# Loads of broadcast decays by halves of the partitions, a reordered token load and two filler products in a fused SSD and MoE kernel

## The chip, the core and the metric

The kernel runs on one core of one Trainium2 chip. The time is device microseconds from launch to end; the span in a profile is from the program's first to its last instruction and is some 1.8 us shorter. Names of engines: PE is TensorE, PEld its weight loads, DVE is VectorE, ACT is ScalarE, POOL is GpSimd, SP the engine that issues most transfers; "SPq" and the like are an engine's sequencer, which issues transfers.

## The reference

A chunked state-space block (Mamba2 SSD) is followed by a mixture of four small two-layer networks:

```python
# attention: x (4, 8, 768, 32), a (4, 8, 768), B and C (4, 8, 768, 16), float32
log_a = np.log(np.clip(a, 1e-06, 1.0))
for c in range(nc):                                   # chunks of 32 tokens
    cum = np.cumsum(la, axis=-1)
    L = np.exp(cum[:, :, :, None] - cum[:, :, None, :]) * causal
    M = np.einsum('bhin,bhjn->bhij', Cc, Bc) * L
    y[:, :, sl] = einsum(M, xc) + einsum(Cc, state) * decay_to_i
    state = decay_full * state + sum over tokens of B x decay_from_j
# mixture: N = 3072 tokens, D = 256, 4 experts, F = 1024
for e in range(E):
    out += p[:, e:e + 1] * (np.maximum(x @ w1[e], 0.0) @ w2[e])
```

The kernel uses chunks of its own, 128 tokens each: 24 of them (chunk 0 to 23), in six blocks (k) of four. The mixture's first products need only chunks 0 and 1; chunks 2 and 3 are computed between them, and the others beside the rest of the mixture. The mixture runs through slices of weights (n = 0, 1, 2, ..., 48 in all); the first two by plain products (lines L618 and L635 of the kernel), the others by a Strassen-like scheme (L569 and L654), which needs sums of weights made by POOL.

## The kernel before

The parts that the change and the argument touch. The decays of a chunk are stored once to DRAM in a cut form `acut_d` [2, 24, 4, 192] and read back with every row repeated over 64 partitions, so that one scan on DVE can make the matrix L (called LT):

```python
    def load_rows(c):                                   # B and C of a chunk, turned
        xb = load.tile([P, OCT + P], FP32, tag="xb", name="xb", bufs=4)
        ...
    def load_x(c, queue=None):                          # its tokens: two transfers of 64 rows
        ...
    def load_decays(c):
        ab = load.tile([P, NQ, TRI], FP32, tag="ab", name="ab")
        nc.sync.dma_start(
            out=ab.rearrange("p q s -> p (q s)"),
            in_=acut_d[:, real(c)].rearrange("t q s -> t (q s)").unsqueeze(1).to_broadcast(
                [NT, HALF, NQ * TRI]))                  # NT = 2, HALF = 64, NQ * TRI = 768
    ...
    def decay_part(c, part):                            # L395
        ...
            nc.vector.tensor_tensor_scan(out=LT[...], data0=s["a"][i], data1=own_i..., ...)
        if part == 1 and c < NCH - CPB:
            nc.gpsimd.tensor_mul(s["MT"][...], halves(c)[...], s["LT"][...])       # L400
    ...
    def turn(n, w=4):                                   # products of ones that only keep PE busy
        for _ in range(n):
            t = ps_att.tile([P, w, P], FP32, tag="att", name="t")
            nc.tensor.matmul(out=t, lhsT=ones, rhs=ones.unsqueeze(1).to_broadcast([P, w, P]), ...)
```

The opening, in the order in which the instructions are written (each engine keeps that order):

```python
    turn(1); turn(1, 2)
    spread(0, banks); turn(1, 3); masks(0)
    scores([0], homes); decays(0); aside(0, 3); store_decays(0)
    masks(1); spread(1, banks); masked([0], (2, 0, 1)); clip_first(nc.gpsimd, 2)
    load_rows(2); load_w1(1); store_decays(1); turn_gates(ps_att, "att")
    load_decays(3)
    outputs([0], ATT); scores([1], ...); decays(1); aside(1, 3)
    load_x(2); load_rows(3); load_w2(0); load_x(3)
    ...                                                 # chunks 2 and 3, first plain products
    load_chunk(4)                                       # rows, tokens, decays, heads
```

## Time and profile before

| | before |
|---|---|
| time, median of 3 runs | 669.06 us (667.31 to 671.33) |
| span of the profiled run | 663.2 us (its time: 664.98 us) |
| PE busy | 641.2 us, 97% of the span |
| PE idle | 22.0 us |
| decays `ab` | 21 loads of 384 KB |

From the page of the kernel before: the span, PE's busy time, then rows of 40 slices of 16.6 us each, where a digit is tenths (PE busy, the clock granted to PE, the busy share of the 16 transfer engines), and the chain of work that ended last:

```profile
span 663.2 us, 10731 instructions
...
PE   8696999999999999999999999999999999999997
...
PEclk8798999999999999999999999999999999999999
DMA  6767754878546486854477855568754687248101
...
PE 77%; DMA 17%; SPq 3%; DVE 2%; issue 1%; POOL 0%; ACT 0%; POOLq 0%; DVEq 0%
```

Apart from the last slice, everything that is not 9 in the rows of PE and its clock lies in the first four slices, 66 us. After them, PE is full in this row. The chain has 17% of its length in transfers. A chain share is not a gain: a link of the chain can be long while PE works beside it.

### The profile page before, as it was taken

Reading aid. Unit: us, or ns where it says so; the run is one execution under the profiler, and the core shown is the slowest. Engines: PE = TensorE matmul, PEld = TensorE weight load, DVE = VectorE, ACT = ScalarE, POOL = GpSimd, SP = SyncE. Lnnn points to the kernel's source line nnn. Section 1 sums busy time; section 2 is a strip of 40 time slices with the busy share of each in tenths; the row PEclk is TensorE's granted clock in tenths of the full one; section 3 lists DMA queues with packets and bytes.
Section 4 is the critical chain, followed back from the end, with each engine's and each line's share of the span. In section 5 each row is a group of like instructions: output and inputs, shape, how many; then the busy total and the mean of one; then the engine's idle time right before and its main releaser. Section 6 shows DMA issues by size and latency. Waiting matters only on the chain.

```text
span 663.2 us, 10731 instructions
## 1 busy us (share of the span) xinstructions
PE 641.2 (97%) x4085; PEld 549.3 (83%) x4085; DVE 470.5 (71%) x814; ACT 124.1 (19%) x314; POOL 106.3 (16%) x169
## 2 busy tenths in 40 slices
PE   8696999999999999999999999999999999999997
PEld 5575888788888888888888888887888888888886
DVE  6353698878868777876687876777767675765665
ACT  4001122121212122122122112212121212111111
POOL 6464455512000001000000100000100000100001
PEclk8798999999999999999999999999999999999999
DMA  6767754878546486854477855568754687248101
GB/s 180 201 211 240 228 181 151 254 284 252 158 139 189 148 267 204 240 141 147 142 205 198 259 164 157 156 178 267 243 173 144 231 270 252 100 129 222 31 1 32
DMA packets 103504, 122.14 MB, mean 184 GB/s; under 512 B 29810, under 2 KB 88478, under 8 KB 103454
## 3 DMA queue, kind: packets, MB, share of 16 engines
q1 hardware_dynamic: 100402, 111.60, 56.8%
q0 software_dynamic: 2432, 9.50, 3.7%
q8 instruction: 32, 0.52, 0.3%
q10 hardware_dynamic: 620, 0.37, 0.2%
q14 instruction: 18, 0.15, 0.1%
HBM read 108.56 MB, written 12.88 MB: 183 GB/s over the span
## 4 chain that ended last, share of the span: by engine, by line
PE 77%; DMA 17%; SPq 3%; DVE 2%; issue 1%; POOL 0%; ACT 0%; POOLq 0%; DVEq 0%
PE acc L654 36%; PE X L569 21%; PE Y L569 16%; DMA ab<-acut_d 6%; DMA wt<-in_w_dram 5%; DMA wt<-w_d 3%; DMA xb<-in_xbc_dram 2%; PE g L429 1%; PE y L488 1%; PE y L466 1%; SPq L136 1%; DMA acut_d<-a_cut 1%; PE acc L635 1%; DVE z L581 0%; DVE hT L598 0%
## 5 line engine op out<-in xcount | busy, mean ns | idle before, releaser
L581 DVE TENSOR_TENSOR z<-Y,snap 128x512 f32<-128x512 f32 x138 | 94.9, 688 | 140.6 <-PE Y L569 75.3
L654 PE MATMUL acc<-hT,wt 128*128 128x256 f32 x736 | 181.0, 379 | 0.0
L576 ACT COPY snap<-X 128x512 f32<-128x512 f32 x138 | 80.8, 586 | 438.8 <-PE X L569 438.8
L654 PEld LDWEIGHTS acc<-hT,wt 128*128 128x128 f32 x736 | 139.8, 190 | 19.0
L654 PE MATMUL acc<-h,wt 128*128 128x256 f32 x552 | 143.6, 383 | 0.0
L569 PE MATMUL X<-yS,wt 128*128 128x256 f32 x552 | 142.6, 381 | 0.0
L569 PEld LDWEIGHTS X<-yS,wt 128*128 128x128 f32 x552 | 105.4, 191 | 14.7 <-issue 0.3
L654 PEld LDWEIGHTS acc<-h,wt 128*128 128x128 f32 x552 | 103.1, 190 | 15.0
L569 PE MATMUL Y<-yT,wt 128*128 128x256 f32 x368 | 95.7, 383 | 6.0 <-DVE z L581 6.0
L591 DVE SCALAR_TENSOR_TENSOR h<-z,gate 128x512 f32<-128x512 f32 x138 | 99.0, 717 | 3.2
L569 PEld LDWEIGHTS Y<-yT,wt 128*128 128x128 f32 x368 | 69.1, 191 | 17.5 <-DVE z L581 7.0
L598 DVE TENSOR_TENSOR hT<-h,hT 128x512 f32<-128x512 f32 x92 | 67.0, 728 | 1.8
L598 DVE TENSOR_TENSOR hT<-h,h 128x512 f32<-128x512 f32 x92 | 61.9, 714 | 1.1
L569 PE MATMUL X<-yT,wt 128*128 128x256 f32 x184 | 47.4, 380 | 3.2 <-issue 1.7
L395 DVE TENSOR_TENSOR_SCAN LT<-ab,own_i 128x384 f32<-128x384 f32 x42 | 39.3, 948 | 13.4 <-DMA ab<-acut_d 13.4
L569 PE MATMUL Y<-yS,wt 128*128 128x256 f32 x184 | 47.2, 379 | 0.0
L591 DVE SCALAR_TENSOR_TENSOR h<-X,gate 128x512 f32<-128x512 f32 x50 | 34.5, 689 | 14.7 <-PE X L618 9.0
L569 PEld LDWEIGHTS X<-yT,wt 128*128 128x128 f32 x184 | 34.7, 190 | 8.9 <-issue 4.3
L400 POOL TENSOR_TENSOR MT<-xb,LT 128x128 f32<-128x128 f32 x20 | 9.9, 495 | 195.9 <-PE Y L569 96.3
L569 PEld LDWEIGHTS Y<-yS,wt 128*128 128x128 f32 x184 | 35.0, 190 | 4.8
L381 POOL TENSOR_TENSOR cts<-xb,dec 128x128 f32<-128x128 f32 x20 | 9.4, 490 | 156.6 <-DVE dec L378 77.2
L441 DVE TENSOR_TENSOR MT<-g,LT 128x192 f32<-128x192 f32 x94 | 26.0, 347 | 3.9 <-PE g L429 3.8
(103 smaller groups left out, 349.9 us busy)
## 6 DMA issues: line engine op xcount, KB each, us to landing
wt<-in_w_dram SPq DMA_DIRECT2D x112, 256.0 KB
wt<-w_d SPq DMA_DIRECT2D x40, 640.0 KB
wt<-w_d SPq DMA_DIRECT2D x40, 512.0 KB
ab<-acut_d SPq DMA_DIRECT2D x21, 384.0 KB
gate<-p_d SPq DMA_DIRECT2D x23, 256.0 KB
w_d<-wt POOLq DMA_DIRECT2D x8, 640.0 KB, 6.8
wt<-in_w_dram SPq DMA_DIRECT2D x40, 128.0 KB
xb<-in_xbc_dram SPq DMA_DIRECT2D x38, 128.0 KB
```

What stands on the lines that cost most here:

```text
L136: queue_.dma_start(out=halves(c)[HALF * t:HALF * t + HALF, :, OX[t]:WX - N * t], in_=src[:, :, t * DM // 2:WX])
L381: nc.gpsimd.tensor_mul(cts, s["xb"][:, OCT:], dec)
L395: nc.vector.tensor_tensor_scan(out=LT[:, i * w:i * w + w], data0=s["a"][i], data1=own_i.rearrange("p q h i -> p (q h i)")[:, :w], initial=0.0,
L400: nc.gpsimd.tensor_mul(s["MT"][:, :, 0:2, HALF:], halves(c)[:, :, OB:].rearrange("p h (q t n) -> p q h t n", q=NQ, t=NT)[:, :, :, 0], s["L ...
L429: nc.tensor.matmul(out=g[:, P * h:P + HALF * h], lhsT=s["btm"][k, h].rearrange("p t j -> p (t j)"), rhs=s["xb"][k, OCT + HALF * h:OCT + P] ...
L441: nc.vector.tensor_mul(s["MT"][:, q, :, :HALF], s["g"][q], s["LT"][:, q])
L569: nc.tensor.matmul(out=f[bank][:, j], lhsT=wt1[n][:, w, j * P:j * P + P], rhs=rhs, start=(i in (1, 2, 5) and j == 0), stop=(j == JJ - 1), ...
L576: nc.scalar.copy(out=s, in_=first[n]["X"])
L581: nc.vector.tensor_add(z, first[n]["Y"], first[n][i])
L591: nc.vector.scalar_tensor_tensor(out=h, in0=first[n][src], scalar=0.0, in1=g.unsqueeze(1).to_broadcast([P, JJ, HB]), op0=ALU.max, op1=ALU. ...
L598: nc.vector.tensor_sub(h[o], h[x], h[y])
L654: nc.tensor.matmul(out=acc[k, u][:, half], lhsT=w2_op(n, w)[:, j], rhs=rhs[:, j], start=(begins and j == 0), stop=(n % SPB == SPB - 1 and ...
```

## The change

Its intent: the decays come by one transfer for each of the two groups of heads (64 partitions each) instead of one for both; the tokens of chunk 2 and the rows of chunk 3 go in front of the decays of chunk 3; and two more products of ones fill places of the opening where PE had nothing to do, to keep its clock up.

```diff
     def load_decays(c):
         ab = load.tile([P, NQ, TRI], FP32, tag="ab", name="ab")
-        nc.sync.dma_start(
-            out=ab.rearrange("p q s -> p (q s)"),
-            in_=acut_d[:, real(c)].rearrange("t q s -> t (q s)").unsqueeze(1).to_broadcast(
-                [NT, HALF, NQ * TRI]))
+        for t in range(NT):
+            nc.sync.dma_start(
+                out=ab[HALF * t:HALF * t + HALF].rearrange("p q s -> p (q s)"),
+                in_=acut_d[t, real(c)].rearrange("q s -> (q s)").partition_broadcast(HALF))
...
     scores([0], homes)
+    turn(1, 2)
     decays(0)
...
     turn_gates(ps_att, "att")
-    load_decays(3)
+    turn(1, 2)
     outputs([0], ATT)
...
     load_x(2)
     load_rows(3)
+    load_decays(3)
     load_w2(0)
```

## The prediction

> **What bounds the kernel now.** I read the page first: the span is 663.2 us and TensorE (PE) is busy 641.2 us of it, so from far away the kernel is bound by matmuls, and all that a change of loads can give back is PE's idle time (663.2 - 641.2 = 22 us) and what PE loses at a low clock. The row PEclk has low digits only in the first slices, and the chain that ended last is 77% PE and 17% DMA. So I went to the opening, the first 70 us, with the timeline of PE and of VectorE (DVE), the waits, and a table of windows. Lines of three engines' timelines (DVE, then PE, then GpSimd, which the trace calls POOL), all those of PE with over 1 us of idle time before them after the start, and one plain line:
>
> ```profile
> 20.80 0.69 DVE L591 SCALAR_TENSOR_TENSOR h<-Y,gate 128x512 f32<-128x512 f32 x1 [0.70 <-PE Y L618]
> 24.51 1.81 DVE L395 TENSOR_TENSOR_SCAN LT<-ab,own_i 128x384 f32<-128x384 f32 x2 [3.02 <-DMA ab<-acut_d]
> ...
> 62.92 0.96 DVE L395 TENSOR_TENSOR_SCAN LT<-ab,own_i 128x384 f32<-128x384 f32 x1 [8.23 <-DMA ab<-acut_d]
> ...
> 26.58 1.09 PE L488 MATMUL y<-MT,xb 64*32 64x144 f32 x32 [5.81 <-POOL MT L400]
> 29.22 3.78 PE L618 MATMUL X<-yT,wt 128*128 128x256 f32 x8
> ...
> 46.00 1.99 PE L618 MATMUL Y<-yT,wt 128*128 128x256 f32 x8 [1.03 <-DVE h L591]
> 64.52 2.08 PE L569 MATMUL Y<-yT,wt 128*128 128x256 f32 x4 [5.16 <-DVE z L581]
> ...
> 25.42 1.11 POOL L400 TENSOR_TENSOR MT<-xb,LT 128x128 f32<-128x128 f32 x1 [10.84 <-DMA xb<-in_xbc_dram]
> ```
>
> The columns are start, length, engine, line, operation, tiles, form, count, and in brackets the idle time before and who ended it. The reader sees three stalls of PE: 5.81, 1.03 and 5.16 us, 12.0 us together. The first goes back to GpSimd (POOL), which waited for the tokens of the third chunk (chunk 2) until 25.4; the other two go back to DVE, which stood in a scan of LT waiting for the decays `ab` of chunks 4 and 5 until 44.3 and 62.9, with the next h and z of PE queued behind it. The waits say the same in total, on the engines and on the issuing queue (columns: us, times, longest):
>
> ```profile
> DVE LT L395 <- DMA ab<-acut_d: 13.4, 3, 8.2
> POOL MT L400 <- DMA xb<-in_xbc_dram: 10.8, 1, 10.8
> ...
> SPq L136 <- DMA ab<-acut_d: 23.2, 5, 5.8
> SPq L175 <- DMA ab<-acut_d: 20.4, 8, 3.2
> ```
>
> The stalls also cost clock. Columns: window, length, busy time and count of each engine, granted clock, DMA share, GB/s:
>
> ```profile
> 20.00:25.00 5.00, 0.77 (x4) 0.34 (x2) 1.28 (x3) 0.00 (x0) 0.00 (x0) 0.94 0.35 101
> 25.00:30.00 5.00, 3.42 (x50) 2.92 (x51) 2.29 (x6) 1.28 (x6) 4.35 (x7) 0.50 0.80 251
> 30.00:35.00 5.00, 5.00 (x15) 3.96 (x14) 0.87 (x2) 0.00 (x0) 4.69 (x7) 0.54 0.89 234
> 35.00:40.00 5.00, 5.00 (x53) 4.11 (x52) 3.89 (x5) 1.10 (x6) 4.43 (x7) 1.00 0.50 160
> ```
>
> The trace's clock records are half speed from 10.73 to 17.55, from 24.38 to 34.62 and from 61.93 to 68.75 us, and full otherwise until the end. And 20 to 25 us has PE idle with DMA only 0.35 busy: nothing computes, and most transfer engines do nothing either, while the loads that everybody waits for are in flight. That is a transfer spread over too few engines. The packets of 3072 bytes are `ab`'s alone (128 a load, one a partition): those of the first load start at 13.44 and end at 23.94 us, with a median of 121 ns each. 128 x 0.121 = 15.5 us of packet time within 10.5 us of clock is fewer than two engines at a time. All 21 loads take 8.5 to 12.6 us so.
>
> **What the Trainium skill says.** The page "DMA: Bandwidth & Descriptors", section "Why a DMA increments its semaphore by 16 and not by 1", says that a transfer uses the largest number of engines up to 16 that divides the slowest dimension of both sides. The source of `ab` is 2 x 64 (a repeat) x 768, so two engines; the trace agrees, as just computed. Its section "Queues, rings and completion order" says that each engine works through its ring of a queue in order. The trace agrees: transfers issued right behind the first `ab` (token loads, w2) landed 11 to 12 us after their issue, at 24.4 to 28 us, where those just before it took 3.5 to 4.7 us; a transfer over 16 engines is complete only when its parts on the two loaded ones are. The same page, "Rules for kernel authors", advises not to split a transfer into disjoint halves of the partitions, as both halves use the same engines. That is no objection here: each half has 64 rows outermost on both sides, so it goes from 2 engines to 16. "TensorE: Matmul & The Clock Gate", Part 1, tells of an idle window that halves the clock and a busy one that restores it; the records above agree (half speed after the idle stretches of 5.81 and 5.16 us, for 10.2 and 6.8 us).
>
> **The change part by part.** (a) Decays by two transfers of 64 x 768. Each of 16 engines gets 8 packets instead of two getting 64: 8 x 0.121 = about 1 us in place of 10.5. No byte is saved; 384 KB a chunk as before, and 21 more issues of some 0.55 us on a queue engine that computes nothing. What is behind in the rings no longer waits. The queue keeps eight transfers in flight (each waits for the eighth before it), so the halves also use up slots, but each lands quickly.
>
> (b) The load of chunk 3's decays goes behind the tokens of chunk 2 and the rows of chunk 3. The former waited on the queue from 10.05 until the store of the cut decays landed at 12.01; the token loads wait only for slots, free at 10.6 and 11.1. So they are issued some 2 us earlier, and at the usual 4 us they land near 15 instead of 25.3. PE comes to the products that need them at 20.76, and GpSimd needs under 0.5 us. The 5.81 us go.
>
> Are the later loads in time? From 13.4 us the queue has to bring, up to and with chunk 4's decays, 4032 KB (tokens and rows 448, ab 384, w2 512, tokens 320, w2, w1, w2 1536, rows and tokens 448, ab 384). At 290 GB/s (an estimate: 5 to 10 us shows 242 GB/s at a share of 0.88, 40 to 45 us shows 314 at 0.89) that is 14.2 us, so 28 us. PE without stalls wants them at about 33. Chunk 5's decays are at 6208 KB, 35 us, with the stores of sums of weights perhaps 39; wanted near 44. So both DVE waits, hence the stalls of 1.03 and 5.16, should go, with 5 us to spare.
>
> (c) Clock. From 26.58 to 34.62 PE is busy about 8.0 us at half speed and from 64.52 to 68.75 about 4.2 us (eight 128x256 products take 3.78 us there, 1.89 in full-speed lines such as the one at 39.62). With no stall there is no drop: 4.0 + 2.1 = 6.1 us back.
>
> (d) The two products of ones, 128x256 each. I take 0.4 us each, an estimate between 0.22 us (eight such products end in 1.89 us when they follow each other) and 0.6 us (in proportion to the 0.91 us that the 128x384 one already there takes). The built order shows the first waiting for DVE (the bank it borrows is read by the first masked product, done near 7.3) and the scores' `a` products for chunk 1 behind it; the second comes before the first outputs, where PE waited anyway (0.35 and 0.10 us). Without an effect on the clock I expect a loss of 0.5 us. If they make the window before 10.73 busy enough, the half speed of 10.73 to 17.55 goes, worth at least the 1.3 us of the first line at 15.16 (3.08 against 1.73) and a part of the small products, together some 1.5 to 2 us. I give that an even chance: half of 1.8, less 0.5, a gain of 0.4 on average.
>
> (e) Later. PE has four more waits: 0.81 us at 107.98, 1.65 at 127.55 (while an `ab` occupies its two engines, 121.5 to 130.1), 0.44 at 348 and 1.07 at 452.8, both for weights. Of these 4.0 us perhaps 2 go.
>
> Sum: 12.0 + 6.1 + 0.4 + 2.0 = 20.5 us; I take 1.3 off for small new waits of PE (for DVE, or GpSimd's sums of weights) when the opening is compressed. 19.2 off 669.06 is 649.9, so 650 us.
>
> **Rivals.** Rival 1: the opening becomes bound by total bandwidth. For it: DMA share is already 0.8 to 0.9 in several windows, and some 11 MB must come in 45 us (245 GB/s). Against it: those shares count packets that queue on two engines, and the sum above leaves 5 us. It would leave some 5 of the 18 us: about 655. Rival 2: GpSimd or DVE takes the place, since PE would reach the third slice of weights (the loop's first) 10 us earlier. For it: GpSimd is busy 4.4 of 5 us from 25 to 40. Against it: its sums of those weights end at 41.4 now and would end near 36, when PE wants them at 41. If it fell behind: 3 to 6 us lost, 653 to 656. Rival 3: the loads are not what held PE and the time stays at 665 to 669; only the queue's slots (21 more transfers) would speak for it, and the idle DMA from 20 to 25 speaks against. Rival 4: all goes well and the clock never drops: 645.
>
> **Range and chances.** Rivals 1 and 2 keep most of the gain, rival 4 adds to it, and the runs of before spread over 4 us, so 644 to 657. Faster by over 2% means under 655.7, that is 13.4 of the 19 us: 0.89. Within 2%: 0.10. Slower by 2%: 0.01, as steady state is untouched.
>
> **What would show it.** Packets of 3072 bytes in bursts of 1 to 3 us; no wait of DVE or GpSimd for `ab` or tokens above 1 us in the opening; PE idle under 3 us from 15 to 70 us; half speed nowhere after 17.6 us; the main loop's matmuls unchanged at 380 ns. PE still idle at 60 us, or an opening with DMA shares of 0.95 and waits for weights, would prove me wrong.

## The result, and the profile after

The changed kernel takes 642.15 us (median of 4 runs, 639.38 to 642.56), the kernel before 668.53 us (4 runs, 667.31 to 671.33). The ratio is 0.9591, with a 95% interval of 0.955 to 0.9632. Ratios here are the mean time of one kernel's fast runs over that of the other's of the same rounds, so not quite the ratio of the medians quoted. The kernel is faster by over 2%, as predicted, but by 26.4 us instead of 19, and 642.15 lies below the range of 644 to 657.

The page of the changed kernel, the same rows:

```profile
span 640.8 us, 10765 instructions
...
PE   8999999999999999999999999999999999999997
...
PEclk9999999999999999999999999999999999999999
DMA  6999778397646568546629745648786854157001
...
PE 98%; DVE 1%; ACT 0%; issue 0%
```

PE is full from the second slice to the last but one, its clock doesn't fall again before the end, and no transfer is left in the chain. The opening's transfers (second to fourth digit of DMA) are now at 9. One caution: the clock row says 9 in the first slice only because the profile's first clock record of this run is at 13.02 us. Durations show that PE was at half speed before it: the filler of 128x384 near 5 us takes 1.65 us here and 0.91 in the trace of before.

The lines of the three timelines that answer to those of the prediction (DVE, then PE, then POOL):

```profile
21.76 1.80 DVE L395 TENSOR_TENSOR_SCAN LT<-ab,own_i 128x384 f32<-128x384 f32 x2
...
44.80 1.48 DVE L395 TENSOR_TENSOR_SCAN LT<-ab,own_i 128x384 f32<-128x384 f32 x1
...
21.05 0.61 PE L488 MATMUL y<-MT,xb 64*32 64x144 f32 x32
22.84 1.99 PE L618 MATMUL X<-yT,wt 128*128 128x256 f32 x8
...
35.78 1.89 PE L618 MATMUL Y<-yT,wt 128*128 128x256 f32 x8
...
48.87 1.03 PE L569 MATMUL Y<-yT,wt 128*128 128x256 f32 x4
...
17.49 0.41 POOL L400 TENSOR_TENSOR MT<-xb,LT 128x128 f32<-128x128 f32 x1
```

None of them has a bracket: no idle time stands before the products that had waited 5.81, 1.03 and 5.16 us, and the eight products of line L618 take 1.99 us in place of 3.78. The stretch from 20 to 70 us as a whole, first before, then after (columns as in the prediction):

```profile
20.00:70.00 50.00, 37.99 (x216) 31.11 (x215) 22.32 (x34) 4.14 (x15) 26.73 (x39) 0.83 0.69 220
```

```profile
20.00:70.00 50.00, 49.82 (x327) 42.65 (x326) 36.88 (x59) 6.97 (x21) 35.22 (x49) 1.00 0.95 292
```

PE is busy 49.82 of 50 us instead of 37.99, at full clock instead of 0.83, and the transfer engines move 292 GB/s instead of 220. The loads of `ab` themselves are in the list of transfers (bytes of one, median us to landing; before, the page told no landing for them):

```profile
ab<-acut_d SPq DMA_DIRECT2D x42, 192.0 KB, 3.2
```

The 3.2 us is the median of only four loads, those whose landing the page could tell. The packed trace holds every update of each load's semaphore, the counter that says when its data has landed. By the last update before the semaphore's next use, the 42 loads landed 4.4 us after their issue in the median (3.1 to 11.6), and the 21 of the kernel before after 12.2 us (10.5 to 16.9).

To see where the time went, I matched the matmuls of the two traces in their order and took, for each, its start in the trace before less its start in the trace after. From 17.6 us on, this lag changes only at these places (until then it swings between 0 and -3.8 us; the first row is what is left of that):

| place in the trace before | lag after it | change |
|---|---|---|
| start to 17.6 us (the new fillers; another phase of the clock) | -0.35 | -0.35 |
| 26.58, outputs of chunk 2 | 5.53 | +5.9 |
| 27 to 34.8, half clock | 9.02 | +3.5 |
| 46.00, Y of a plain product | 10.22 | +1.2 |
| 64.52, Y of the first Strassen slice | 15.65 | +5.4 |
| 65 to 68.5, half clock | 17.71 | +2.1 |
| 107.98, 127.55, 348.46, 452.83 | 22.71 | +5.0 |

### The profile page after: what moved, and what is told of

It is laid out like the page before. It is cut to its first block, busy times and chain, and to the rows that moved or that the text cites. A ratio compares the mean times of both kernels' runs of the same rounds, so it can differ in the third digit from the quotient of the medians.

```text
span 640.8 us, 10765 instructions
## 1 busy us (share of the span) xinstructions
PE 634.4 (99%) x4089; PEld 544.9 (85%) x4089; DVE 470.2 (73%) x814; ACT 124.2 (19%) x314; POOL 109.0 (17%) x169
## 4 chain that ended last, share of the span: by engine, by line
PE 98%; DVE 1%; ACT 0%; issue 0%
PE acc L654 44%; PE X L569 25%; PE Y L569 19%; PE acc L635 2%; PE g L429 2%; PE y L488 2%; PE X L618 1%; PE Y L618 1%; PE y L466 1%; PE t L776 1%; PE a L362 0%; PE gp L337 0%; DVE qmask L270 0%; ACT yT L501 0%; DVE a_q L279 0%
## 5 line engine op out<-in xcount | busy, mean ns | idle before, releaser
L569 PE MATMUL Y<-yT,wt 128*128 128x256 f32 x368 | 94.4, 379 | 0.0
L400 POOL TENSOR_TENSOR MT<-xb,LT 128x128 f32<-128x128 f32 x20 | 9.5, 473 | 187.7 <-PE Y L569 86.2
L395 DVE TENSOR_TENSOR_SCAN LT<-ab,own_i 128x384 f32<-128x384 f32 x42 | 40.7, 982 | 0.0
```

Of the source, the lines that this page charges most:

```text
L395: nc.vector.tensor_tensor_scan(out=LT[:, i * w:i * w + w], data0=s["a"][i], data1=own_i.rearrange("p q h i -> p (q h i)")[:, :w], initial=0.0,
L569: nc.tensor.matmul(out=f[bank][:, j], lhsT=wt1[n][:, w, j * P:j * P + P], rhs=rhs, start=(i in (1, 2, 5) and j == 0), stop=(j == JJ - 1), ...
```

## The experiments

Twelve kernels ran in four jobs, each job on one chip and beside the kernel before. All gave correct results. "PE waits" are the idle times of PE after 20 us in the profiled run, over 0.3 us, without the 0.3 us at the very end that all have. The medians of the kernel before were 664.61, 665.03, 664.62 and 668.0 us in the four jobs, with single runs from 662.3 to 671.4, so only ratios are compared across jobs.

| run | median us (runs) | ratio, 95% interval | PE waits, us |
|---|---|---|---|
| c0_before | 666.73 (6) | 1.0015 (0.9979 to 1.0052) | 5.5, 1.2, 7.5, 2.4 |
| e1_split_only | 643.67 (6) | 0.9667 (0.9633 to 0.9702) | none |
| e2_order_only | 666.73 (4) | 1.002 (0.9968 to 1.0072) | 3.3, 5.2, 2.8, 0.35, 1.5, 0.33, 2.5 |
| e3_turns_only | 667.29 (4) | 1.0023 (0.9977 to 1.0068) | 8.5, 1.3, 6.2, 1.1, 1.3, 1.6, 2.2 |
| c1_after | 643.81 (6) | 0.9679 (0.9648 to 0.971) | none |
| e4_no_turns | 642.8 (6) | 0.9667 (0.9643 to 0.9691) | none |
| e5_four_on_two | 672.74 (4) | 1.0117 (1.0088 to 1.0147) | 2.2, 5.0, 4.3, 0.56, 1.9, 3.5, 3.1 |
| e6_split_early | 641.9 (6) | 0.9672 (0.9633 to 0.9712) | none |
| e7_split_late | 659.74 (6) | 0.9921 (0.9887 to 0.9954) | 1.8, 4.5, 2.8, 0.52 |
| e8_four_on_sixteen | 644.61 (3 fast) | 0.9689 (0.9647 to 0.9732) | not compared |
| e9_three_and_seven | 652.76 (4) | 0.9814 (0.9775 to 0.9854) | 2.4, 3.9, 0.42 |
| e10_wide_turns | 643.23 (6) | 0.9609 (0.9575 to 0.9643) | none |

### The two controls

c0_before is the kernel before, c1_after the changed one, unchanged.

> The kernel before, unchanged, as a control, to have the granted clock of every timed run. The traces of the first two profiles account for 22.4 us (663.2 to 640.8), the medians differ by 26.4. If the profiled run of before was a lucky one in its clock (mean 0.982), the timed runs at 667 to 671 should show lower mean clocks, 0.975 or less; if the clocks are the same 0.98, the extra 3 to 4 us are stalls or something that the profile does not show. Time: 668, ratio 1.00.

The six runs had mean clocks from 0.977 to 0.990, and the eleven runs of the same kernel beside them 0.979 to 0.990. The clock doesn't order the times: runs at 0.990 took from 662.7 to 669.02 us. So my guess that the profiled run of the prediction had been lucky in its clock is not borne out. The waits differ from run to run: here the third stall was 7.5 us where the first trace had 5.16, and there was one late wait, not four. Matched in the same way, this trace ends 2.3 us behind the first one, and it falls behind at the third stall. That run-to-run part of the kernel before (some 9 us from the fastest to the slowest of all its runs) is not explained further.

> The changed kernel, unchanged, as a control on the chip of the next three: 642 us, ratio 0.96, mean clock 1.00 in the records.

643.81 us against 665.03: the gain is 21.2 us in this job and was 26.4 in the first rounds.

### Which part of the change does it: one part alone

e1_split_only has only the new body of `load_decays`. e2_order_only has only these lines, e3_turns_only only the two `turn(1, 2)`:

```diff
     turn_gates(ps_att, "att")
-    load_decays(3)
     outputs([0], ATT)
...
     load_rows(3)
+    load_decays(3)
     load_w2(0)
```

> Decays by two transfers of 64 rows, chunk 3's decays still in front of chunk 2's tokens, no products of ones. Theory E (the two-engine transfers held everything): the tokens are issued only after 12 us but land near 17, before PE wants them at 21, so nearly all of the gain is here: 641 to 645 us. Rival O (the order did much of it): 648 to 656, with PE idle before the outputs of chunk 2. Rival C (the products of ones keep the clock): a half-speed stretch near 10 to 17 us comes back, mean clock under 0.99, 644 to 648.

643.67 us: the two transfers alone give the whole gain, as far as these runs resolve it. The tokens of chunk 2 are ready at 19.18 us (POOL's line waits 3.38 us for them), and PE doesn't feel it. In this run the clock rose only at 20.5 us, so it doesn't test rival C; e4 does.

> Tokens and rows in front of chunk 3's decays, each load of decays still one transfer on two engines, no products of ones. Theory E: the first stall of PE (5.8 us) goes, but the decays of chunk 3 then land near 26 us and PE waits for them before the outputs of chunk 3, and the stalls at 46 and 64 us and the late ones stay: 662 to 668 us. Rival O: 650 to 657.

666.73 us, no gain. The trace shows why: the first stall has only moved from chunk 2 to chunk 3, whose tokens now stand behind the slow decays. PE's timeline of this run:

```profile
28.78 0.71 PE L488 MATMUL y<-MT,xb 64*32 64x144 f32 x32 [3.27 <-POOL MT L400]
45.23 3.78 PE L618 MATMUL Y<-yT,wt 128*128 128x256 f32 x8 [5.22 <-DVE h L591]
63.79 2.07 PE L569 MATMUL Y<-yT,wt 128*128 128x256 f32 x4 [2.80 <-DVE z L581]
```

These are 3.27 + 5.22 + 2.80 = 11.3 us, against 12.0 before. PE came earlier to each place and waited there.

> The two products of ones alone. Theory E: they cost up to 0.7 us of PE in the opening and cannot help the stalls near 21 and 60 us: 667 to 670. Rival C: the half-speed stretch of 10.7 to 17.6 us goes and 1.5 to 2 us with it: 665 to 667, mean clock up by 0.005.

667.29 us, no gain. But the products do what they are for. In this run the clock rose at 4.0 us, as in the trace of before (3.9), so the two have the same phase and can be compared. First before, then this run:

```profile
10.80:17.50 6.70, 6.65 (x66) 4.98 (x64) 2.79 (x7) 2.69 (x10) 3.23 (x7) 0.50 0.72 203
```

```profile
11.04:17.80 6.76, 6.76 (x95) 5.31 (x91) 4.44 (x12) 2.70 (x10) 3.14 (x5) 1.00 0.63 183
```

The clock (the number before the DMA share) stays at 1.00. PE starts the last of the eight products that stand at 15.16 in the trace before 2.5 us earlier than there. Then it waits for the same late tokens, 8.5 us instead of 5.8:

```profile
26.73 1.09 PE L488 MATMUL y<-MT,xb 64*32 64x144 f32 x32 [8.51 <-POOL MT L400]
```

### What the products of ones are worth when the loads are fast

e4_no_turns is the changed kernel without them; e10_wide_turns has them twice as wide, `turn(1, 4)`.

> The changed kernel without its two products of ones. Rival C (they keep the clock up): a half-speed stretch of 6.8 us appears in the first 20 us in most runs, mean clock 0.995 or lower, 643.5 to 645.5 us. If they do nothing for the clock: 641.5 to 642.5, as they cost some 0.5 us at a place where PE waits in part.

642.8 us (641.96 to 643.87), against 643.81 (640.61 to 646.08) for the changed kernel in the same rounds: no difference that these runs resolve, and none in favour of the products. In the profiled run the drop of the clock was there, 0.50 from 11.04 to 17.87 us, and its span was 640.3 us. Two things offset each other. If PE's clock is high early, the products keep it high (the 2.5 us of e3). If it is still low, they run at half speed (1.22 us for the first in the changed kernel's trace, 0.70 in e3's) and push everything back. Across the traces with fast loads and these or wider products, the span roughly follows when the clock became full: at 8.2 us 638.8 us (c1), at 12.5 us 641.3 (e10), at 13.0 us 640.8 (the first trace), at 20.6 us 643.1 (e6). The mean clocks of the timed runs fit this: the three runs of e4 at 0.994, which is what the traced one with the drop has, took 641.96 to 642.06 us, and the three at 0.999, so without it, 643.53 to 643.87. When the clock rose in runs that were not traced is not on record, so the offset is likely but not shown.

> The changed kernel with its two new products of ones twice as wide (128x512). The traces so far order the time by when the clock first becomes full for good: 8 us (638.8 us span), 13 us (640.8), 20.5 us (642.2 and 643.1), and the run without products of ones lost it again from 11 to 18 us (640.3). If wider products make an earlier window busy in every phase, the clock is full by 14 us in all runs, and the spread shrinks: 640 to 642.5 us. If they only cost time at half clock (0.4 to 0.9 us each): 643.5 to 645.5 us.

643.23 us, 640.03 to 643.75, a ratio of 0.9609 beside a kernel before that was slower than elsewhere (668.0). The spread is 3.7 us, against 5.5 in c1 and 3.2 in the first rounds, so no shrinking can be told from these few runs. One run was traced, with the clock full at 12.5 us; whether it was full by 14 us in all six is not shown. It is no better version; nor is any other run here clearly better than the changed kernel.

### Is it the number of engines or the number of transfers

In e5 and e8 each half of 64 rows comes by two transfers. In e5 they have 62 and 2 rows, in e8 32 and 32, in e9 57 and 7:

```diff
         for t in range(NT):
-            nc.sync.dma_start(
-                out=ab[HALF * t:HALF * t + HALF].rearrange("p q s -> p (q s)"),
-                in_=acut_d[t, real(c)].rearrange("q s -> (q s)").partition_broadcast(HALF))
+            for lo, hi in ((0, CUT), (CUT, HALF)):          # CUT = 62, 32 or 57
+                nc.sync.dma_start(
+                    out=ab[HALF * t + lo:HALF * t + hi].rearrange("p q s -> p (q s)"),
+                    in_=acut_d[t, real(c)].rearrange("q s -> (q s)").partition_broadcast(hi - lo))
```

> The changed kernel, but each half of 64 rows is loaded by a transfer of 62 and one of 2 rows. 62 has no divisor up to 16 above 2, so if the number of engines follows the divisor rule each of the four runs on two engines. Theory E: 3072-byte packets stretch over some 10 us again and the stalls for decays come back: 660 to 672 us (the tokens still go first, and four transfers take four of the eight slots). If the splitting itself, and not the number of engines, made the gain: 641 to 645.

672.74 us, slower than the kernel before. The packets of 3072 bytes of a load again stretch over 9.2 to 13.5 us, with a sum of packet time of 16 to 22 us, so at most some two packets at a time, as two engines would give. All stalls are back, and the late waits are the largest seen. From the waits of this run (us, times, longest; its line numbers are one higher from L152 on):

```profile
PE X L570 <- DMA wt<-in_w_dram: 6.7, 2, 3.5
PE Y L619 <- DVE h L592: 5.0, 1, 5.0
PE Y L570 <- DVE z L582: 4.8, 2, 4.3
```

> Each half of 64 rows by two transfers of 32 rows (16 engines each): as many transfers and slots as the run with 62 and 2 rows, but all engines. If the number of engines is what matters: 642 to 646 us, with bursts of 3072-byte packets of 3 to 6 us. If the number of transfers in the eight slots made that run slow: 655 or more.

Its three fast runs took 644.61, 646.41 and 642.27 us: as many transfers as e5, all engines, and the gain is there. A fourth run, the profiled one, was 949.71 us at a granted clock of 0.66; it is left out. In it, too, the packets of the first two loads of `ab` took 3.2 and 4.0 us. So it is the engines, and three fast runs show no cost of four transfers in place of two when they land fast (the interval of the ratio, 0.9647 to 0.9732, holds that of the changed kernel in another job, 0.9679). That they cost more when they are slow (e5 is 1% above e2, with the same order of loads) fits the eight slots of the queue, but no run separates it.

> Each half of 64 rows by a transfer of 57 (57 = 3 x 19, so three engines by the divisor rule) and one of 7 (seven engines). On the busiest engine 2 x 19 + 2 = 40 packets of 3072 bytes in place of 64, at 0.121 us each 4.8 us in place of 7.7. A load should take some 5 to 7 us from first to last packet, and the time should lie between two and sixteen engines: 643 to 655 us; if five us of slack are enough, at the low end.

652.76 us, between the two, and the loads took 4.9 to 12 us (the first three 6.9, 7.6 and 11.0). I had thought that five microseconds of slack would cover this. They don't: PE waits 2.43 and 3.93 us in the opening. The second wait goes back to the decays of chunk 4 themselves, for which DVE stood 4.63 us, until 37.52. For the first, the slack of the decays was not the smallest one. The tokens of chunk 3, which come behind the decays and w2, landed at 21.6 and 22.2 us in the changed kernel by their semaphore records, and POOL used them at 23.69: 1.5 us. In e9 POOL had to wait for them until 25.6 (L401 there is L400 of the others, as the edit has one line more):

```profile
25.60 0.41 POOL L401 TENSOR_TENSOR MT<-xb,LT 128x128 f32<-128x128 f32 x1 [6.93 <-DMA xb<-in_xbc_dram]
```

The semaphores show the number more directly, and alike in all loads of a kernel. A load on few engines has one update 0.4 to 1.6 us after its issue and then a few as it lands; the later ones are read here as one for each engine. The first load of the kernel before has them at 13.08 and then at 23.94 and 24.42 us. Updates at landing, for one transfer:

| transfer | kernels | updates at landing |
|---|---|---|
| 2 x 64 rows | before, c0, e2, e3, and the single transfers of e6 and e7 | 2 |
| 62 rows; 2 rows | e5 | 2; 2 |
| 57 rows; 7 rows | e9 | 3; 7 |
| 64 rows | changed kernel, c1, e1, e4, e10, and the split ones of e6 and e7 | 16 |
| 32 rows | e8 | 16 |

They also show how others were held up. The first of the two token loads of chunk 2 in the trace before was issued at 12.70 us; fourteen of its sixteen updates had come by 17.18, and the last two came at 24.45 and 24.91, right behind those of `ab`.

### Where the late waits come from

e6_split_early uses the two transfers for chunks 3 to 7 and the old single one from chunk 8 on; e7_split_late the other way round:

```diff
+        if c < 8:                  # e7: c >= 8
             for t in range(NT):
                 ...                # two transfers
+        else:
+            ...                    # one transfer, as before
```

> The changed kernel, with two transfers only for the decays of chunks 3 to 7; from chunk 8 on one transfer over two engines as before. The aligned traces put 5.0 us of the gain after 100 us (1.1 before chunk 8's decays are used, 3.9 with them: waits of PE for weights at 127, 348 and 453 us of the trace before). If those waits are the two-engine transfers delaying weights, this loses 3 to 4 us: 645 to 646. If they came from something else in the opening: 642.

641.9 us: four runs at 641.8 to 641.9, one at 644.88 (the profiled one, whose clock rose late) and one at 648.79. Nothing is lost in the median. The trace has the late loads stretching over 8.3 to 12.6 us, two engines as before, and PE does not wait at all after 120 us:

```profile
120.00:635.00 515.00, 514.89 (x3237) 447.19 (x3236) 375.79 (x641) 99.60 (x241) 28.77 (x48) 1.00 0.58 176
```

The run at 648.79 was not traced to this depth, so a late wait in it can't be excluded; its mean clock of 0.995, where the others have 0.999 or 1.000, says that it lost the clock for a while.

> The opposite of the run with two transfers for chunks 3 to 7 only: chunks 3 to 7 by one transfer on two engines, two transfers from chunk 8 on. The former run showed that late two-engine loads after a clean opening cost nothing. If the late waits of PE for weights (near 127, 350 and 455 us) are an after-effect of the slow opening alone, they stay: 664 to 667 us, waits of 3 us or more after 120 us in the trace. If they need both a queue that runs late and two-engine loads in front of the weights, they go: 660 to 663 us, no wait of PE above 0.5 us after 200 us.

659.74 us: the opening is nearly as slow as before (its three stalls have 9.1 us in place of 12.0, and PE is 2.2 us ahead at the wait of 107.98), and yet the late waits are gone; after the wait of 0.52 us at 105.78 there is none:

```profile
120.00:635.00 515.00, 514.89 (x3263) 446.93 (x3262) 378.95 (x652) 99.06 (x240) 36.22 (x58) 1.00 0.59 186
```

The same stretch of the kernel before, for comparison:

```profile
120.00:635.00 515.00, 511.73 (x3245) 443.39 (x3244) 378.68 (x647) 98.87 (x240) 41.84 (x65) 1.00 0.63 189
```

So, by one trace each, the late waits need both: slow loads in the opening and two-engine loads later. Removing either removes them. In the trace before, the issuing queue reached the load of chunk 17's decays at 335.7 us, 12.8 us before PE's wait for weights; in e6, it did so at 315.0, 15.0 us before the same matmul (330.0). That the weights behind the slow load are in time because the queue is 2.2 us earlier is my reading, not a test. What keeps the queue late for 250 us after a slow opening I have not shown.

## Why the prediction was right or wrong

The mechanism was right. The steps that failed are terms of the sum: the gain late in the run, (e), and the 1.3 us taken off for new waits were mis-sized, and the traced losses were taken off a time that they did not belong to. In (b) the right number was put down to the wrong part of the change.

**The cause was right.** A load of `ab` ran on two engines; e5, e8 and e9 show it by changing only how rows are cut into transfers, and the semaphores count it. (The working by packets was a little off: the median of the first load's packets is 128 ns, not 121, which is that of all loads, and they add up to 21.1 us in 10.5, so two at a time and not fewer.) e1 shows that this alone gives the gain. The chain from it to PE (tokens and decays late, DVE and POOL stand, PE waits, its clock falls) is the one predicted, and its effects on PE are in the table of lags.

**Part (a), two transfers.** "About 1 us in place of 10.5" was too good. Bursts took 2 to 6.4 us from first to last packet in the changed kernel, probably because other transfers share the engines, which no run tests. It was enough: the loads landed after 4.4 us in the median instead of 12.2.

**Part (b), the order.** The tokens landed at 15.13 and 15.71 us, near the 15 predicted, though they were issued only 0.85 us earlier (11.85 in place of 12.70), not 2. But it was not the order that saved PE: e1 has them in time without it, and e1 and e4, which differ just by it, have the same ratio to the kernel before (0.9667, in two jobs). I had credited the 5.81 us to this part; they belong to the number of engines. e2 shows what I had not thought through: with slow decays, the reorder only moves the stall to the next chunk.

**The three stalls.** 12.0 us predicted; the lags give 5.9 + 1.2 + 5.4 = 12.5.

**Part (c), the clock.** 6.1 us predicted, 3.5 + 2.1 = 5.6 found.

**Part (d), the products of ones.** I gave them +0.4 us on average at even chances; the first trace lost 0.35 by 17.6 us, and c1 shows no gain over e4. That they can hold the clock, which I left open, is shown by e3.

**Part (e), the late waits.** This step failed by its size: "perhaps 2 go" of 4.0, and 5.0 us went (the lag counts up to 0.3 us more at a place than the wait). The forecast gave no reason for keeping half of them; e6 and e7 show that the slow transfers are needed twice for them, early and late, and the change removes both. The amount isn't an accident of one trace: matched against the control c0_before, the same stretch gives 4.5 us, there one wait of 2.4 us and a stretch at half clock from 130.45 to 133.87.

**The sum.** "I take 1.3 off for small new waits": there were none above 0.18 us after 12 us. Together with (e) this makes the 19.2 us 3 us too small for the traces (22.4); the other parts come to -0.75 (stalls +0.5, clock -0.5, products of ones -0.75). The rest of the miss is the base: I took the losses from a trace whose own run took 664.98 us and subtracted them from the median of 669.06. Another 3.5 us (the profiled run against the median of 668.53) thus were losses that this trace did not show and that I left standing in the result. Which they were in those runs is not known; in c0's trace, of a run of 667.3 us, the third stall alone was 2.4 us longer. The controls and the other jobs, with ratios of 0.967 to 0.968 in the first two jobs, where the kernel before had medians of 664.6 and 665.0, say that the gain was 21 to 22 us there; the 26.4 of the first rounds probably hold some of the spread of the kernel before.

**The rivals.** Rival 1 (total bandwidth) came closer than I allowed: 20 to 70 us ran at a DMA share of 0.95 and 292 GB/s, almost exactly the 290 I had estimated, with only 1.5 us of slack for the tokens of chunk 3. Rival 2 did not happen: POOL was busy 35.2 of the 50 us, and PE never waited for it. Rival 3 is excluded by e1. Rival 4 ("all goes well", 645) is nearest to what happened, and was still 3 us too high.

## What to carry to other kernels

When everybody waits for loads while most transfer engines are idle, look at the outermost dimension of both sides of the load: here a repeat over 2 x 64 rows confined it to two engines, as 62 rows did in e5, and it delayed all that was queued behind. Reordering around such a load only hands the wait to the next one; make it use all engines first. And where the change removes the very losses that differ from run to run, subtract what a trace shows from the time of that trace's run, not from the median of others (664.98 less 22.4 is 642.6; measured 642.15).

## What the Trainium skill lacked or had wrong

- "DMA: Bandwidth & Descriptors", Rules for kernel authors: the row against splitting a transfer over halves of the partitions takes for granted that both halves use all 16 engines anyway, and doesn't say when the undivided transfer does not. Here the split alone gave 643.67 against 664.61 us. (The row "Use all 16 engines" of the same table does cover the case; the two don't refer to each other.)
- "TensorE: Matmul & The Clock Gate", Part 1, speaks of idle and busy windows, and does not say how busy is busy. PE was busy 5.49 of 6.70 us from 4.0 to 10.7 us in the trace before, with small products of 32 rows among them, and the clock was still halved at 10.7; in e3, with two more products of 128x256 and 5.53 of 6.70 us busy (4.3 to 11.0), it was not; and in e4, without them, it was halved at 11.04 though PE was busy 5.72 of the same 6.70 us. So the share of busy time in the records doesn't tell whether the clock stays; what does is open.
- The same Part 1 warns that clock records in a profile can be unreliable, but not that they may begin late: the changed kernel's first is at 13.02 us, earlier windows print 1.00, and durations there are those of half speed (1.65 against 0.91 us).
